# Copies of h in the last four units of a gated MLP beside attention: two parts each, at once

## The chip, the cores and the metric

The kernel runs on one core of one Trainium2 chip. The metric is the device time of that core in microseconds, here the median of three runs. Every number of the profile comes from one execution that the hardware profiler recorded.

## What is computed

An attention block and a bilinear gated MLP share one normalised input; the MLP gates the attention.

```python
xn = layernorm(x)                                  # x: 2048 x 576
q, k, v = split(xn @ wqkv)                         # 32 heads of 18
s = concat(softmax(q @ k.T * 18 ** -0.5) @ v) @ wo
h = (xn @ w_gate) * (xn @ w_up)                    # 2048 x 4608
g = silu(h @ w_down)
return x + s * g
```

All of it is in fp32. Where the kernel needs the accuracy, it splits a number into a rounded high part and a rest and adds three products (high by high, high by rest, rest by high).

## The kernel before

**Tiles and streams.** The MLP goes in 72 units: four chunks of 512 tokens by 18 blocks of 256 hidden columns (`units`). A unit has two halves, n = 2u and 2u + 1, of 128 hidden columns each. TensorE's 128 rows are used as two halves of 64 rows, each with a stream of its own: stream 0 gives the up products and stream 1 the gate products (27 matmuls a half, 512 columns, line 703), and both give down products (48 a unit, 288 columns, line 749). The order in each stream is: gate or up of unit u, then the down products of unit u − 1. Where both streams have work, their matmuls overlap.

**Where h goes.** At the end of a gate half (`gate_end`) VectorE multiplies gate and up (L715), ScalarE writes the high part of h to `hs` (L719) and GpSimd the rest (L720). The down products sum over 64 rows at a time, so each stream needs both halves of the rows: one lies in `hs`, the other in `hx`, a copy of `hs` with its upper and lower 64 partitions exchanged. SyncE issues that copy as two DMAs (`turn_round`, L739). For units 1 to 69 the copy of unit u is issued in `down_end`, behind the last down product of unit u − 1 in both streams, since there is one buffer `hx`; the load of wd for unit u (`d_get`, L240) is issued just ahead of it. For units 70 and 71 the copy goes in two parts, one at the end of each gate half, unit 70 into a buffer `hxl` in the place of the first accumulators `acc` and unit 71 into `hx`.

**The attention beside it.** 2048 score products for the maxima (a, L624, on stream 0) and 2048 for the exponentials (b, L656, on stream 1, for the last head on stream 0 as well) are set between the MLP's matmuls. ScalarE takes the exponentials (L658) into 29 buffers `pt`. When seven blocks of four stand there, both streams stop for a visit: the products with V (L667, `pv_group`), which free the buffers. The last blocks go in two visits of four. When a head is whole, VectorE divides it (L679 to L684) and its rows go to DRAM (`sot`, L687); behind the last visit they are loaded again as `o` (L843) for the final product with wo (L1295), which VectorE multiplies with the gate (L1304).

**What sets the order.** The whole order of the main part is written when the program is built, by a planner (`order`, line 1157) with clocks of its own for the two streams, the engines and SyncE's queue (`moved`: bytes at 0.24 MB/us, and 2.0 us). It gives the next instruction to the stream whose clock is behind. `can_go` (line 1118) holds a stream's first down product of unit n back until `there["h", n]` and `downed[n - 1]` are past, the planner's times at which the copy of h and the load of wd have landed. A score product b is given when its goal has passed. The goals are 0.75 us apart for the last 88 (`LAST`, line 975), and they are shifted by the lead of stream 0 in issued MLP work:

```python
lean = PULL * (gone[0] - gone[1] - SKEW) * (1 if r else -1)      # line 1185; PULL 3.0, SKEW 3.0
```

A 512-column matmul counts 0.2285 us (`LONG`), a 288-column one 0.1325. SyncE issues its DMAs in the order of the program and waits at each for what it needs.

Of the kernel before, what the change touches and what calls it, by code (L numbers as in the profile page):

```python
# [40 lines left out]
def kernel(  # L41
# [564 lines left out]
    with ExitStack() as mid:  # L606
# [103 lines left out]
        def gate_end(n, ps):  # L710
            u, j = divmod(n, 2)
            if j == 0:
                hs[u] = gp.tile([128, 2, 2, 512], FR, name="hs", bufs=2)
            h32 = us.pop(n)
            nc.vector.tensor_tensor(h32, ps, h32, op=OP.mult)  # L715
            if g_after(n):
                g_get(g_after(n))
            hj = hs[u][:, j]
            nc.scalar.activation(hj[:, 0, :], h32, AF.Copy)  # L719
            nc.gpsimd.tensor_tensor(hj[:, 1, :], h32, hj[:, 0, :].bitcast(FT), op=OP.subtract)  # L720
            if u == 0 or u >= len(units) - 2:
                turn_round(u, j)

        hx = {}

        def turn_round(u, j):

            if u >= len(units) - 2:
                if j == 0 and u == len(units) - 2:
                    hx[u] = accp.tile([128, 2, 2, 512], FR, name="hxl", tag="acc")  # L730
                elif j == 0:
                    hx[u] = gp.tile([128, 2, 2, 512], FR, name="hx", bufs=1)
                js = slice(j, j + 1)
            else:
                if u or j == 0:
                    hx[u] = gp.tile([128, 2, 2, 512], FR, name="hx", bufs=1)
                js = slice(0, 2) if u else slice(j, j + 1)
            for r in range(2):
                nc.sync.dma_start(hx[u][half[r], js].bitcast(FT), hs[u][half[1 - r], js].bitcast(FT))  # L739
# [28 lines left out]
        def down_end(r, u, s, ps):  # L768
            c, q = units[u]
            cs = slice(r * HALF, (r + 1) * HALF)  # L770
            if q == 0 and c >= 2:
                ready(sdone, 4 * c - 8 + s)
            a = sums(4 * c + s)[:, cs]
            if q == 0:
                nc.vector.tensor_copy(a, ps[:, 0:HALF])  # L775
            else:
                nc.vector.tensor_tensor(a, a, ps[:, 0:HALF], op=OP.add)  # L777
            if q == NF2 - 1 and c < NCH - 1:
                seen[c, s] = seen.get((c, s), 0) + 1
                if seen[c, s] == 2:  # L780
                    silu_store(4 * c + s)
            if s == 3:
                seen[u] = seen.get(u, 0) + 1
                if seen[u] == 2:
                    d_get(u + 1)
                    if u + 1 < len(units) - 2:
                        turn_round(u + 1, 1)

        def silu(t, new, end):
# [367 lines left out]
        def order():  # L1157
            nonlocal na, nb
            load_v(0)
            g_get(2)  # L1160
            feeds = [stream(0), stream(1)]
            heads.extend(next(f) for f in feeds)
            wait = None
            while any(heads) or na < TOTAL or nb < TOTAL or due:
                now = max(clk)
                small(now)
                if nb == TOTAL and not lo:
                    begin()
                if nb == TOTAL and len(banks["g"]) == 4:
                    banks["g"] += [max(banks["a"])] * 2  # L1170
                if loads and queue[0] <= now + 0.3:
                    f, a, size_mb = loads.pop(0)
                    f(*a)
                    moved(now, size_mb)
                need = size(due[0]) if due and (nb < TOTAL or any(heads) and not stuck[0]) else 1
                if len(due) >= need and due[need - 1][2] <= now:
                    wait = now if wait is None else wait
                    if abs(clk[0] - clk[1]) < 0.04 or now > wait + 1.0 or not all(heads):
                        visit(now if any(heads) else max([now] + [d[2] for d in due]))
                        wait = None  # L1180
                        if nb == TOTAL and not due:
                            prefetch(now)
                        continue
                r = 0 if clk[0] <= clk[1] else 1
                lean = PULL * (gone[0] - gone[1] - SKEW) * (1 if r else -1)

                if r == 0 and (na < TOTAL or nb < TOTAL - N) or r == 1 and nb == 0 and na < N:
                    at, goal, score, can = next_free("a"), a_goal(na) + lean, a_next, na < TOTAL and na < nb + N + MOST and stacked(0, na)
                    can = can and not late(goal, r)
                    at += LOAD if goal > clk[r] - BEHIND else 0.0  # L1190
                else:
                    at, goal, score, can = next_free("b"), b_goal(nb) + lean, b_next, b_ready(r)
                op = heads[r]
                held = op is not None and not can_go(r, op[1], op[4])
                stuck[0] = held and heads[1 - r] is not None and not can_go(1 - r, heads[1 - r][1], heads[1 - r][4])
                if held:
                    op = None
                blocked = op is not None and op[1] and next_free("g") > clk[r]
                if can and (at <= clk[r] + 0.01 and (goal <= clk[r] or blocked) or op is None and (at <= clk[r] or not held)):
                    clk[r] = max(clk[r], at)  # L1200
                    score(r)
                elif op is not None:
                    length, first, work, end, (kind, n, k) = op
                    if first:
                        clk[r] = max(clk[r], next_free("g"))
                        slots[r] = banks["g"].index(next_free("g"))
                        banks["g"][slots[r]] = 1e9
                    work()
                    lands = issue(r, length)
                    gone[r] += length  # L1210
                    if end:
                        done = engine(end[0], lands, end[1])
                        banks["g"][slots[r]] = done + EARLY
                        if kind == "d":
                            if k == 47:
                                parts.setdefault(n, []).append(clk[r])
                                if len(parts[n]) == 2:
                                    downed[n] = moved(max(parts[n]) + 0.3, 1.18) if (n + 1) % NF2 and n + 2 < len(units) else 0.0
                                    if n + 3 < len(units):
                                        there["h", n + 1] = moved(max(parts[n]) + 1.0, 1.05)  # L1220
                        elif r == 0:
                            upped[n] = done
                        else:
                            gated[n] = done
                            fin = engine("ACT", done + 0.05, 0.535)
                            fin = engine("POOL", fin + 0.05, 1.29)
                            if n != 2:
                                anew = 4 * NF2 - UNSAVED <= g_after(n) < 4 * NF2
                                loaded[g_after(n) - 2] = moved(done - 0.4, 1.18) if (n // 2 + 1) % NF2 and not anew else 0.0
                            if n // 2 >= len(units) - 2:  # L1230
                                there["h", n // 2] = moved(fin, 0.524) - (0.0 if n // 2 < len(units) - 1 else 1.1)
                            elif n < 2:
                                there["h", 0] = moved(fin, 0.524)
                            for _ in range(2):
                                hot = n + 2 >= 2 * NF2 and n % (2 * NF2) in (34, 35, 0) and n + 2 < 2 * len(units)
                                for want in stacks:
                                    if hot and (want[0] is load_pair or n % (2 * NF2) == 2 * NF2 - 1):
                                        continue
                                    stacks.remove(want)
                                    send(want, fin + 1.4)  # L1240
                                    break
                    heads[r] = next(feeds[r], None)
                else:
                    clk[r] = max(clk[r] + 0.05, min(clk[1 - r] + 0.01, clk[r] + 0.3))
# [120 lines left out]
```

## Time and profile before

| | |
|---|---|
| median of 3 runs | 2565.24 us |
| lowest and highest | 2562.74 and 2565.86 us |
| profiled execution | 2566.68 us |
| its span in the trace | 2564.9 us |
| matmuls busy | 2544.2 us (99%) |
| weight loads busy | 2115.4 us (82%) |
| VectorE busy | 1933.2 us (75%) |
| ScalarE busy | 1473.1 us (57%) |
| granted TensorE clock | 0.999 |

Times in the trace count from the start of the span. PE is TensorE's matmuls, PEld its weight loads, DVE VectorE, ACT ScalarE, POOL GpSimd, and SPq the queue of SyncE, which issues most DMAs. L703 is line 703 of the kernel. A name such as `hx<-hs` says what is written from what.

### The profile page before, as it was taken

How to read it: one execution, taken by the hardware profiler on the slowest of the kernel's cores; microseconds unless marked ns; L12 is line 12 of the kernel's file. 1: busy time of each engine (PE TensorE's matmuls, PEld its weight loads, DVE VectorE, ACT ScalarE, POOL GpSimd, SP SyncE). 2: the span in 40 equal slices, each digit the busy share in tenths (PEclk: the TensorE clock that was granted, in tenths of full speed). 3: DMA queues.
4: the chain of work that ended last, by engine and by line, in shares of the span. 5: the costliest groups of instructions: out<-in, count | busy, mean ns of one | idle time of the engine just before them, and what ended most of it. 6: DMA issues, size and time to landing. Idle time of an engine off the chain costs nothing.

```text
span 2564.9 us, 59227 instructions
## 1 busy us (share of the span) xinstructions
PE 2544.2 (99%) x24360; PEld 2115.4 (82%) x24360; DVE 1933.2 (75%) x3377; ACT 1473.1 (57%) x2712; POOL 618.9 (24%) x687
## 2 busy tenths in 40 slices
PE   8999999999999999999999999999999999999998
PEld 7899888787888888878888888778888888888878
DVE  6208678877778888777878888777889887778537
ACT  5222666666666655556666665555656656556651
POOL 3214334443421111112311111111111121111125
PEclk9999999999999999999999999999999999999999
DMA  7796889889775656576766566565666666664567
GB/s 246 234 293 163 222 220 244 222 217 248 199 222 173 183 174 185 173 183 186 214 201 174 172 178 184 168 178 154 180 204 164 175 190 176 178 175 142 160 194 248
DMA packets 203979, 499.87 MB, mean 195 GB/s; under 512 B 57744, under 2 KB 125200, under 8 KB 165948
## 3 DMA queue, kind: packets, MB, share of 16 engines
q1 hardware_dynamic: 193020, 482.86, 66.7%
q0 software_dynamic: 9952, 11.74, 1.7%
q8 instruction: 192, 3.15, 0.5%
q10 hardware_dynamic: 736, 1.47, 0.2%
q14 instruction: 79, 0.65, 0.1%
HBM read 307.49 MB, written 107.61 MB: 162 GB/s over the span
## 4 chain that ended last, share of the span: by engine, by line
PE 95%; DMA 2%; DVE 2%; ACT 0%; SPq 0%; POOL 0%; issue 0%; ACTq 0%; DVEq 0%
PE pg L703 35%; PE pg L667 17%; PE pg L749 15%; PE pa L624 11%; PE pb L656 9%; PE pg L423 2%; PE pa L368 2%; PE pb L368 2%; PE pg L1295 1%; DVE mx L626 0%; DMA sqk<-hl 0%; PE pa L1295 0%; PE pb L1295 0%; DMA hx<-hs 0%; DMA xi<-in_A_x_dram 0%; DMA gin<-sg 0%
## 5 line engine op out<-in xcount | busy, mean ns | idle before, releaser
L626 DVE TENSOR_REDUCE mx<-pa 128x1 f32<-128x512 f32 x2048 | 1364.7, 686 | 222.7 <-PE pa L624 114.1
L658 ACT ACTIVATE pt<-pb 128x512 f32<-128x512 f32 x2048 | 1160.8, 598 | 532.9 <-PE pb L656 477.2
L703 PE MATMUL pg<-xc,wgu 64*128 64x512 f32 x7722 | 1358.1, 388 | 0.0
L703 PEld LDWEIGHTS pg<-xc,wgu 64*128 64x128 f32 x7722 | 1048.2, 184 | 36.0 <-DVE acc L775 0.2
L656 PE MATMUL pb<-pair,ring 64*128 64x512 f32 x2016 | 784.6, 395 | 2.6 <-DMA pair<-mt 2.6
L624 PE MATMUL pa<-pair,ring 64*128 64x512 f32 x2008 | 778.2, 393 | 1.1 <-DVE mx L626 1.1
L749 PE MATMUL pg<-wd,hs 64*128 64x288 f32 x3408 | 582.2, 292 | 0.3 <-DVE acc L777 0.2
L749 PE MATMUL pg<-wd,hx 64*128 64x288 f32 x3360 | 567.7, 292 | 0.0
L749 PEld LDWEIGHTS pg<-wd,hs 64*128 64x128 f32 x3408 | 489.0, 185 | 5.5 <-issue 0.8
L720 POOL TENSOR_TENSOR hs<-us,hs 128x512 fp32r<-128x512 f32 x144 | 186.3, 1293 | 1262.6 <-ACT hs L719 1251.5
L749 PEld LDWEIGHTS pg<-wd,hx 64*128 64x128 f32 x3360 | 477.9, 185 | 3.0
L667 PE MATMUL pg<-pt,vt 128*32 128x512 f32 x4096 | 454.8, 594 | 1.0 <-DVE acc L777 0.9
L624 PEld LDWEIGHTS pa<-pair,ring 64*128 64x128 f32 x2008 | 364.9, 184 | 68.3 <-issue 51.1
L656 PEld LDWEIGHTS pb<-pair,ring 64*128 64x128 f32 x2016 | 366.0, 184 | 9.5 <-issue 2.9
L667 PEld LDWEIGHTS pg<-pt,vt 128*32 128x32 f32 x4096 | 125.5, 110 | 284.7 <-issue 278.3
L777 DVE TENSOR_TENSOR acc<-acc,pg 128x288 f32<-128x288 f32 x544 | 231.6, 443 | 26.4 <-PE pg L749 22.7
L673 DVE TENSOR_TENSOR oc<-oc,pg 128x512 f32<-128x512 f32 x69 | 47.2, 685 | 217.3 <-PE pg L667 217.2
L719 ACT ACTIVATE hs<-us 128x512 fp32r<-128x512 f32 x144 | 91.0, 632 | 140.2 <-DVE us L715 139.2
L206 POOL TENSOR_TENSOR wgu<-wraw,wgu 128x384 fp32r<-128x384 f32 x129 | 129.5, 1020 | 98.3 <-ACT wgu L205 81.5
L671 ACT ACTIVATE oc<-pg 128x512 f32<-128x512 f32 x32 | 19.1, 598 | 188.3 <-PE pg L667 181.8
L646 POOL DMA_DIRECT2D pair<-mt x128 | 77.9, 614 | 178.5 <-DVE mt L641 171.9
L715 DVE TENSOR_TENSOR us<-pg,us 128x512 f32<-128x512 f32 x144 | 98.5, 684 | 26.3 <-PE pg L703 18.0
(147 smaller groups left out, 1394.4 us busy)
## 6 DMA issues: line engine op xcount, KB each, us to landing
wgu<-swg SPq DMA_DIRECT2D x94, 1152.0 KB
hx<-hs SPq DMA_DIRECT2D x138, 512.0 KB
wd<-swd SPq DMA_DIRECT2D x50, 1152.0 KB
swg<-wgu SPq DMA_DIRECT2D x36, 1152.0 KB
pair<-sqk SPq DMA_DIRECT2D x192, 144.0 KB
ring<-sqk SPq DMA_DIRECT2D x384, 72.0 KB
swd<-wd SPq DMA_DIRECT2D x18, 1152.0 KB
sqk<-hl SPq DMA_DIRECT2D x32, 512.0 KB
```

The lines of the kernel that those rows point to most:

```text
L206: nc.gpsimd.tensor_tensor(w[:, 9 + b:12 + b, :], raw[:, b:b + 3, :], w[:, b:b + 3, :].bitcast(FT), op=OP.subtract)
L368: nc.tensor.matmul(p, wq[b, a], xcs[c][:, e, :], start=n == 0, stop=n == len(PAIRS) - 1)
L624: nc.tensor.matmul(p, q[rows, t * 128:(t + 1) * 128], k[rows, c * 512:(c + 1) * 512], start=True, stop=True)
L626: nc.vector.tensor_reduce(mx[h][:, t, c:c + 1], p, axis=AX.X, op=OP.max)
L656: nc.tensor.matmul(p, k[rows, t * 128:(t + 1) * 128], q[rows, c * 512:(c + 1) * 512], start=True, stop=True)
L658: nc.scalar.activation(pt[t, c], p, AF.Exp, scale=scale)
L667: nc.tensor.matmul(p[32 * c:32 * c + 32, :], vt[h // 2][:, t, 6 * (h % 2):6 * (h % 2) + 32], pt[t, c], start=t == ts[0], stop=t == ts[-1])
L703: nc.tensor.matmul(ps, gw[n][half[r], a, :], xg[i][half[r], e, :], start=k == 0, stop=k == len(TERMS) - 1)
L715: nc.vector.tensor_tensor(h32, ps, h32, op=OP.mult)
L720: nc.gpsimd.tensor_tensor(hj[:, 1, :], h32, hj[:, 0, :].bitcast(FT), op=OP.subtract)
L749: nc.tensor.matmul(ps[:, 0:HALF], (hx if k else hs)[u][half[r], j, a, s * 128:(s + 1) * 128], dw[u][half[r], k, j, e, :], start=n == 0, st ...
L777: nc.vector.tensor_tensor(a, a, ps[:, 0:HALF], op=OP.add)
```

## The change

The copy of h in two parts, one at the end of each gate half, now holds for the last four units (68 to 71), not the last two. The even ones of them go into the buffer of the first accumulators, the odd ones into `hx`. The planner's times for the copies follow.

```diff
-            if u == 0 or u >= len(units) - 2:
+            if u == 0 or u >= APART:
                 turn_round(u, j)
 
         hx = {}
+        APART = len(units) - 4
 
         def turn_round(u, j):
 
-            if u >= len(units) - 2:
-                if j == 0 and u == len(units) - 2:
+            if u >= APART:
+                if j == 0 and u % 2 == 0:
                     hx[u] = accp.tile([128, 2, 2, 512], FR, name="hxl", tag="acc")
                 elif j == 0:
                     hx[u] = gp.tile([128, 2, 2, 512], FR, name="hx", bufs=1)
...
                 if seen[u] == 2:
                     d_get(u + 1)
-                    if u + 1 < len(units) - 2:
+                    if u + 1 < APART:
                         turn_round(u + 1, 1)
...
                                     downed[n] = moved(max(parts[n]) + 0.3, 1.18) if (n + 1) % NF2 and n + 2 < len(units) else 0.0
-                                    if n + 3 < len(units):
+                                    if n + 1 < APART:
                                         there["h", n + 1] = moved(max(parts[n]) + 1.0, 1.05)
...
-                            if n // 2 >= len(units) - 2:
+                            if n // 2 >= APART:
                                 there["h", n // 2] = moved(fin, 0.524) - (0.0 if n // 2 < len(units) - 1 else 1.1)
```

## Rows read from the trace of the kernel before

**Rows 1.** The page, section 1: busy us (share of the span) xinstructions.
```profile
PE 2544.2 (99%) x24360; PEld 2115.4 (82%) x24360; DVE 1933.2 (75%) x3377; ACT 1473.1 (57%) x2712; POOL 618.9 (24%) x687
```
**Rows 2.** Windows: busy us (xinstructions) of PE, PEld, DVE, ACT, POOL, clock, DMA share, GB/s.
```profile
2430.20:2440.70 10.50, 10.50 (x101) 10.46 (x98) 0.85 (x2) 8.88 (x18) 0.00 (x0) 1.00 0.69 184
2440.80:2443.70 2.90, 2.90 (x16) 2.35 (x13) 0.69 (x1) 2.52 (x5) 1.29 (x1) 1.00 0.94 243
```
**Rows 3.** TensorE in order of time from 2440.8: start us, us, instructions merged.
```profile
2440.83 0.84 PE L703 MATMUL pg<-xc,wgu 64*128 64x512 f32 x3
...
2443.75 0.40 PE L749 MATMUL pg<-wd,hs 64*128 64x288 f32 x1
```
**Rows 4.** TensorE in order of time from 2412.1.
```profile
2412.13 0.39 PE L656 MATMUL pb<-pair,ring 64*128 64x512 f32 x1
...
2413.05 0.39 PE L749 MATMUL pg<-wd,hs 64*128 64x288 f32 x1
```
**Rows 5.** SyncE's queue in order of time, units 68 and 69 and the tail.
```profile
2386.73 1.06 SPq L265 DMA_DIRECT2D ring<-sqk  x3
2402.32 0.34 SPq L240 DMA_DIRECT2D wd<-swd  x1
2402.77 1.40 SPq L739 DMA_DIRECT2D hx<-hs  x2
...
2418.61 1.05 SPq L265 DMA_DIRECT2D ring<-sqk  x3
2432.63 0.34 SPq L240 DMA_DIRECT2D wd<-swd  x1
2433.09 1.11 SPq L739 DMA_DIRECT2D hx<-hs  x2
...
2487.81 2.94 SPq L687 DMA_DIRECT2D sot<-oc  x4
```
**Rows 6.** Windows behind three issues of copies; the last number is GB/s.
```profile
2403.20:2412.90 9.70, 9.70 (x86) 9.53 (x83) 1.92 (x6) 6.44 (x12) 5.88 (x9) 1.00 1.14 247
2433.50:2443.10 9.60, 9.60 (x77) 9.13 (x74) 0.69 (x1) 8.03 (x16) 0.80 (x1) 1.00 1.00 259
2477.70:2480.20 2.50, 2.50 (x33) 2.42 (x31) 0.44 (x1) 1.89 (x4) 0.00 (x0) 1.00 0.98 247
```
**Rows 7.** Waits of SyncE's queue, 2380 to 2520: us in total, times, longest.
```profile
SPq L739 <- POOL hs L720: 11.6, 4, 4.3
SPq L687 <- DVE oc L684: 3.9, 1, 3.9
```
**Rows 8.** TensorE in order of time: the first product of the last head's exponentials.
```profile
2416.90 0.47 PE L656 MATMUL pb<-ring,pair 64*128 64x512 f32 x1
```
**Rows 9.** GpSimd in order of time: the last silu that reads the first accumulators.
```profile
2094.14 1.42 POOL L805 TENSOR_TENSOR sil<-sil,acc 128x576 f32<-128x576 f32 x1 [8.05 <-DVE sil L802]
```
**Rows 10.** Windows of pt alone: PE, PEld and ACT busy (x); ACT is the exponentials.
```profile
2405.50:2412.00 6.50, 0.00 (x0) 0.00 (x0) 2.78 (x5) 1.00 1.08 256
2412.00:2416.90 4.90, 0.00 (x0) 0.00 (x0) 3.46 (x7) 1.00 0.92 208
2428.10:2448.80 20.70, 0.02 (x3) 0.02 (x4) 15.49 (x28) 1.00 0.69 191
```
**Rows 11.** The chain that ended last, in order of time: start us, us, what.
```profile
2483.01 8.33 DMA hx<-hs
...
2491.41 0.34 SPq L843
...
2513.25 0.47 DVE ys L1304
```
**Rows 12.** TensorE in order of time, the final products; in brackets the idle time.
```profile
2513.86 1.03 PE L1295 MATMUL pa<-wos,hi 128*128 128x288 f32 x6 [1.22 <-DVE ys L1304]
```
**Rows 13.** ScalarE in order of time, the last exponentials.
```profile
2474.85 3.85 ACT L658 ACTIVATE pt<-pb 128x512 f32<-128x512 f32 x6
2479.07 0.60 ACT L658 ACTIVATE pt<-pb 128x512 f32<-128x512 f32 x1
```

## The prediction

> **What bounds the kernel now.** The page's busy times come first: the matmul row is full nearly from end to end, and everything else is below it [rows 1]. That says only that TensorE never stands empty, not that it works at its full rate, since two matmuls on the two halves of its rows overlap. So the second view is the busy times by windows round the units that the diff touches, cut so that no visit of the P·V products lies in them. The reader is to look at the weight loads (PEld) in it. With both streams at work 98 of them take 10.5 us, 107 ns each; from 2440.8 on 13 take 2.9 us, 223 ns each, though the matmul row is full in both [rows 2]. Here one stream runs alone. The third view, TensorE's instructions in order of time, shows which: from 2440.83 only products of gate and of scores come, until the first down product (L749) at 2443.75 [rows 3]. The same is seen in small from 2412.13 to 2413.05 [rows 4]. The fourth view, SyncE's queue, says why. The copy of h of units 68 and 69 is issued only when the down products of the unit before are all through, behind the load of wd: wd at 2402.32 and the copy at 2402.77, wd at 2432.63 and the copy at 2433.09 [rows 5]. Both together are 1.18 + 1.05 = 2.23 MB, and at the 247 and 259 GB/s of the windows that follow they take 9.0 and 8.6 us [rows 6]. From the start of those windows that is 2412.2 and 2442.1, close ahead of the two first down products. The planner has counted the same (`there["h", ...]`), and holds the down products of stream 0 back until then. So the profile has two holds that this change can remove, 0.92 and 2.92 us of one stream.
>
> A rule bears on how such a hold is priced. In the longer one the matmul row is busy 2.90 us of 2.90, the weight loads 2.35 [rows 2]. The Trainium skill (Perfetto Trace Analysis, section Identifying the Most-Contended Engine) calls the first no good measure of the distance to the roofline and the second a good one. By the first the hold would be worth 0, by the second 2.90 − 2.35 = 0.55 us; the count of loads, 223 ns apart against 107, gives half of the hold, 1.5 us, and the trace decides for the count.
>
> **What the change does, part by part.** Ahead of unit 68 no line of the program differs, so nothing moves before its gate halves, the second of which stands ahead of the load of ring at 2386.73 [rows 5]. Only the last 190 us are in play.
>
> (a) *Copies of units 68 and 69 go early.* They leave at the ends of the gate products as those of unit 70 do today, and no longer after the down products of the unit before. They are there more than 15 us ahead of their use. Both holds go: half of 0.92 and half of 2.92 us, −0.5 and −1.5, together **−1.9 us of TensorE** (rounded from 1.92).
>
> What is late next at those places is wd. Alone its 1.18 MB need 1.18/0.247 = 4.8 us from 2403.2, so 2408.0, and 1.18/0.259 = 4.6 us from 2433.5, so 2438.1 [rows 6]. Stream 0 arrives at 2412.1 and 2440.8; the slack is 4 and 2.7 us. By the planner's own sum (0.3 + 1.18/0.24 + 2.0 = 7.2 us after the down products) the second is 2439.8, 1.0 us ahead. I cost that at nothing, at most 1 us of one stream, 0.5 us, if stream 0 leads by more.
>
> (b) *Four issues of 256 KB in place of two of 512 KB a unit.* SyncE needs 1.11 us for two, so 2.2 us more in all. SyncE also now waits there for GpSimd's subtraction, as in the four waits of units 70 and 71 (11.6 us in all, the longest 4.3) [rows 7]. Queued behind are the loads of ring for head 31, today at 2386.73 and 2418.61 [rows 5]; they go at most 4.3 + 1.1 = 5.4 us later. The first product of head 31 with those rows comes at 2416.90 [rows 8], and the second half of ring is wanted 32 products later, beyond 2440 by 0.74 us each. The cover is 24 and 16 us; without it each microsecond would go to the score products. Cost 0. The halves are no slower for their bytes: 247 GB/s for a pair of halves, 259 GB/s for the two whole ones with wd [rows 6].
>
> (c) *The other buffer.* hx of unit 68 takes the place of the first accumulators, last read by the last silu of the third chunk, which GpSimd ends at 2095.56 [rows 9], 280 us before. hx of 69 takes that of 67, whose down products are through at 2402.3. Neither is a wait. Cost 0.
>
> (d) *The planner's pace of score products.* No wait and no instruction is added here, but it is the term that I think decides. Stream 1 gives a score product whenever its goal is due, and the goal is put off by 3 us for each microsecond by which stream 0 has issued more than stream 1 (line 1185). While stream 0 runs freely, each product on stream 1 costs it 0.2285 us, so the pace is 0.75 + 3 × 0.2285 = 1.44 us a product. The trace shows five exponentials in 6.5 us ahead of the hold, 1.30 each, and seven in 4.9 us once stream 0 is held [rows 10]. The hold itself buys them: 3 × 0.92 = 2.8 us of goal. Without it, 4.9/1.30 = 3.8 products fit into those 4.9 us, so **3 products are put off**. From 2416.9 on both streams may give products of head 31, and the pace is that of ScalarE and two score banks: 28 in 20.7 us, 0.74 each [rows 10]. Nothing there is idle enough to catch up, so the last exponential comes 3 × 0.74 = **2.2 us later**. The bounds: nothing, if they are caught up; 7 × 1.30 − 4.9 = 4.2 us, if all seven go at the old pace.
>
> (e) *What ends the tail.* Behind the last product the last P·V visit, its division, the stores of head 31's rows (2487.81, where the queue waited 3.9 us for VectorE) and the loads of o (2491.41) follow one after the other, and the chain runs on through gin, xi and o to 2513.25 [rows 5, 7, 11]. TensorE already waits 1.22 us there [rows 12]. So the 1.9 us of (a) do not reach the end: earlier down products only make that wait longer. What they bring is that the copy of unit 71, which lands at 2491.34 [rows 11] and holds the first load of o, is out of the way by the stores' end, today 2487.81 + 2.94 = 2490.75: −0.6 us. Bounds of that: 0 and −1.9.
>
> **The sum.** −1.9 us on TensorE, absorbed by the wait of (e); +2.2 by (d); −0.6 by (e): +1.6 us. The profiled execution took 2566.68 us (span 2564.9 and 1.8 around it), 1.4 above the median of 2565.24; it would come to 2568.3, and the median to **2566.8 us**. That is 0.06%, and 0.2% (5.1 us, about what a measurement of this kernel can tell from no change) is beyond all the terms but one bound.
>
> **The rivals.**
> *The gain arrives.* If the score products are caught up, or stream 0 takes more of them, the last exponential comes 1.9 us earlier with everything else: 2565.2 − 1.9 = 2563.3. For it: the planner balances the streams, and the last products stand on both. Against: ahead of the last exponential, which ends at 2479.67, ScalarE gives six of them end to end in 3.85 us, so it has no room there to be sooner [rows 13]. The Trainium skill (Perfetto Trace Analysis, section DMA Optimizations) says that DMAs split into smaller chunks may start sooner and let the whole task end sooner; it would give this rival; the rows bear it out for the two holds, and none does for the end.
> *Slower.* All seven products go at 1.30 us, head 31 begins 4.2 us late, and at the end gate and up are done while products remain: they run alone at half rate, half of 4.2 − 1.9, so 1.1 us more. 4.2 + 1.1 = +5.3: 2570.5. It decides from four put-off products on. For it: stream 0's lead feeds on itself through line 1185. Against: from 2416.9 on stream 0 takes products too, which ends it.
> *It does not do what it says.* With more lead, stream 0 meets the load of wd (slack 1.0 us by the planner) or of the next gate weights, and is held there instead: 0, so 2565.2.
>
> **How the numbers follow.** Forecast 0.45, gain 0.27, slower 0.18, held elsewhere 0.10. The forecast and the last one are within 0.2%; of the gain, 0.05 is for a last stretch that also closes its 1.22 us wait and more; of the slower case two thirds, 0.12, lie beyond 0.2%, since its 5.3 us leave out what is lost when visits move too. So faster 0.05, same 0.83, slower 0.12. The range reaches from the gain, less half the distance of the shown runs' lowest from their median (2565.24 − 2562.74 = 2.50), so 2562.0, to the slower case, 2570.5.
>
> **What would show it.** In the trace after: no stretch of L703 and L656 alone ahead of the first down products of units 68 and 69 (a); four copies at gate ends, ring issued behind them (b); exponentials still about 1.3 us apart between 2412 and 2417, and a next P·V visit that begins later than before (d); the first load of o behind head 31's stores (e). If that visit begins earlier or the last exponential ends before 2479.67, (d) is wrong and the gain arrives. If the loads of o move and the end does not, (e) is wrong.

## The result, and the profile after

The changed kernel takes 2572.82 us (median of 8 runs, 2567.73 to 2574.42), the kernel before 2564.62 (8 runs): a ratio of 1.003, 95% interval 1.0022 to 1.0039. It is slower by 8.2 us, and above the range of the prediction. The profiled execution of the changed kernel took 2570.59 us, with a span of 2568.8. That is 2.2 us below its median, and the profiled execution of the kernel before (2566.68 us) lies 2.1 above its own. So the two traces are 3.9 us apart, and they show the cause at work but only about half of the 8.2 us.

The two holds are gone. Windows of the changed kernel at the places of [rows 2] (columns as there): the weight loads now fill the stretch round unit 69's first down products (the first begins at 2439.93), 28 in 2.9 us against 13.

```profile
2430.70:2437.30 6.60, 6.60 (x61) 6.24 (x61) 0.45 (x1) 6.11 (x12) 0.00 (x0) 1.00 0.60 212
2437.40:2440.30 2.90, 2.90 (x30) 2.90 (x28) 0.69 (x1) 2.10 (x5) 1.10 (x1) 1.00 0.49 153
```

TensorE in order of time, to be held against [rows 4]: the first down products of unit 68 now follow the dense gate and up products at once.

```profile
2410.46 1.52 PE L703 MATMUL pg<-xc,wgu 64*128 64x512 f32 x11
2411.73 0.39 PE L656 MATMUL pb<-pair,ring 64*128 64x512 f32 x1
2411.82 0.42 PE L750 MATMUL pg<-wd,hs 64*128 64x288 f32 x2
```

SyncE's queue, to be held against [rows 5]: the copies go in parts behind the loads of gate weights, and a load of ring waits behind one of them (2390.04, before 2386.73). Head 31's stores come at 2494.38, before 2487.81, and the loads of o behind them.

```profile
2380.60 1.10 SPq L740 DMA_DIRECT2D hxl<-hs  x2
2385.97 0.33 SPq L197 DMA_DIRECT2D wgu<-swg  x1
2388.89 1.10 SPq L740 DMA_DIRECT2D hxl<-hs  x2
2390.04 2.02 SPq L265 DMA_DIRECT2D ring<-sqk  x3
...
2494.38 1.37 SPq L687 DMA_DIRECT2D sot<-oc  x4
2495.99 2.28 SPq L844 DMA_DIRECT2D o<-sot  x5
```

The exponentials alone by windows, as in [rows 10] (the last bracket before the clock is their count): 5 in 4.9 us in the place of the seven, then 9 (one of them begun before) in 7.7 us until the next P·V visit, which begins at 2424.3. Behind that visit 28 take 22.1 us, before 20.7.

```profile
2405.10:2411.60 6.50, 0.00 (x0) 0.00 (x0) 2.77 (x5) 1.00 0.43 114
2411.60:2416.50 4.90, 0.00 (x0) 0.00 (x0) 2.48 (x5) 1.00 0.91 318
2416.50:2424.20 7.70, 0.00 (x0) 0.00 (x0) 4.49 (x9) 1.00 0.74 224
2430.60:2452.70 22.10, 0.00 (x0) 0.00 (x0) 15.76 (x28) 1.00 0.66 219
```

And here is what the prediction did not see. ScalarE in order of time, to be held against [rows 13]: the last gate half is over at 2476, ScalarE then issues the six loads of wo, and 13 exponentials (4 + 2 + 4 + 3) stand behind them in its queue. The first waits 3.56 us. Before, those issues came at 2480.55, behind the last exponential.

```profile
2475.11 1.08 ACT L658 ACTIVATE pt<-pb 128x512 f32<-128x512 f32 x2 [3.34 <-PE pb L656]
2476.14 0.63 ACT L719 ACTIVATE hs<-us 128x512 fp32r<-128x512 f32 x1
2476.15 1.84 ACTq L826 DMA_DIRECT2D wor<-in_A_wo_dram  x4
2478.03 2.26 ACTq L828 DMA_DIRECT2D wor<-in_A_wo_dram  x2
2480.34 2.27 ACT L658 ACTIVATE pt<-pb 128x512 f32<-128x512 f32 x4 [3.56 <-DMA wor<-in_A_wo_dram]
2482.78 1.09 ACT L658 ACTIVATE pt<-pb 128x512 f32<-128x512 f32 x2 [0.17 <-PE pb L656]
2484.03 2.32 ACT L658 ACTIVATE pt<-pb 128x512 f32<-128x512 f32 x4 [0.15 <-PE pb L656]
2486.52 1.78 ACT L658 ACTIVATE pt<-pb 128x512 f32<-128x512 f32 x3 [0.17 <-PE pb L656]
```

TensorE stands as well, for 3.31 us until the first of these exponentials is through; down products go on at that moment too, which fits a queue in order whose head waits for a score bank. In the windows it has 0.01 us of work between 2478 and 2481. After the last down product it waits for o, and from 2500 to 2506.8 the granted clock is 0.50, the lower of its two levels, 1.2 GHz.

```profile
2480.99 0.49 PE L656 MATMUL pb<-ring,pair 64*128 64x512 f32 x1 [3.31 <-ACT pt L658]
2480.99 0.40 PE L750 MATMUL pg<-wd,hs 64*128 64x288 f32 x1
...
2478.00:2481.00 3.00, 0.01 (x2) 0.01 (x2) 0.00 (x0) 0.66 (x2) 0.13 (x1) 1.00 0.98 302
2497.60:2500.00 2.40, 0.79 (x6) 0.37 (x2) 1.63 (x4) 0.88 (x2) 0.00 (x0) 0.99 0.92 278
2500.00:2506.80 6.80, 6.21 (x24) 5.67 (x24) 1.96 (x2) 2.00 (x4) 4.59 (x3) 0.50 0.98 281
```

The chain of waits, to be held against [rows 11] and [rows 12]: it goes through the issues of wo and the exponential behind them, which the chain before does not, and then through the load of o, the rounding of o on ScalarE and the final products at half clock.

```profile
2476.58 0.44 ACTq L826
2477.07 3.27 DMA wor<-in_A_wo_dram
2480.34 0.61 ACT pt L658
...
2495.99 3.12 DMA o<-sot
2499.12 0.63 ACT hi L852
...
2500.90 3.01 PE pa L1296 x10
```

Three places measure the tail. The early parts of the executions differ by up to 4 us, so I count each from the start of the P·V visit near 2391 us, which stands ahead of every matmul and exponential that the change moves (the times are read from the order of time):

| from that visit, us | last exponential ends | product of the last gate half begins (L715) | last final product begins |
|---|---|---|---|
| before | 88.0 | 88.1 | 166.7 |
| changed | 97.0 | 84.1 | 171.5 |

Before, the first two lie within 0.1 us of each other. The change moves the MLP 4.0 us forward and the exponentials 9.0 us back.

### The profile page after: what moved, and what is told of

Same layout as the page of the kernel before. It is cut to its first block, busy times and chain, and to the rows that moved or that the text cites. A ratio compares the mean times of both kernels' runs of the same rounds, so it can differ in the third digit from the quotient of the medians.

```text
span 2568.8 us, 59234 instructions
## 1 busy us (share of the span) xinstructions
PE 2545.2 (99%) x24360; PEld 2114.8 (82%) x24360; DVE 1931.2 (75%) x3377; ACT 1472.0 (57%) x2712; POOL 617.3 (24%) x687
## 4 chain that ended last, share of the span: by engine, by line
PE 96%; DVE 2%; DMA 1%; ACT 0%; POOL 0%; issue 0%; ACTq 0%; DVEq 0%; SPq 0%
PE pg L703 35%; PE pg L667 18%; PE pg L750 16%; PE pa L624 11%; PE pb L656 9%; PE pg L423 2%; PE pa L368 2%; PE pb L368 2%; PE pg L1296 1%; PE pa L1296 1%; PE pb L1296 1%; DVE mx L626 0%; DMA sqk<-hl 0%; DMA pair<-mt 0%; DVE st L298 0%; DVE us L715 0%
## 5 line engine op out<-in xcount | busy, mean ns | idle before, releaser
L750 PE MATMUL pg<-wd,hx 64*128 64x288 f32 x3312 | 558.3, 292 | 0.0
L750 PEld LDWEIGHTS pg<-wd,hx 64*128 64x128 f32 x3312 | 470.1, 185 | 2.9
L715 DVE TENSOR_TENSOR us<-pg,us 128x512 f32<-128x512 f32 x144 | 98.5, 684 | 20.8 <-PE pg L703 18.9
```

The lines of the kernel that those rows point to most:

```text
L750: nc.tensor.matmul(ps[:, 0:HALF], (hx if k else hs)[u][half[r], j, a, s * 128:(s + 1) * 128], dw[u][half[r], k, j, e, :], start=n == 0, st ...
```

## The experiments

Each run is compared with the kernel before on the same chip; intervals are 95%.

**Copies or order.** Two halves of the change. First the copies alone:

```diff
-                                    if n + 1 < APART:
+                                    if n + 3 < len(units):
...
-                            if n // 2 >= APART:
+                            if n // 2 >= len(units) - 2:
```

> The changed kernel with the planner's two lines as before: the copies of units 68 and 69 go early and in parts, but every matmul and every exponential stands in the order of the kernel before, the down products held back included. Theory 'order': the loss of 8.2 us lies in the new order alone, so this is the time of the kernel before, 2564.6 us, within 2 us. Rival 'copies': the extra issues, SyncE's waits for GpSimd or the shared buffer cost, so this stands near the changed kernel's 2572.8 us.

Measured: 2564.97 us, ratio 1.000 (0.9991 to 1.0009). Then the kernel before with the changed planner's times alone:

> The kernel before with the planner's two lines of the change: the matmuls and exponentials stand in the order of the changed kernel, but the copies of units 68 and 69 still go whole and behind the down products of the unit before. Theory 'order': 2572.8 us and up to 4 us more, since the first down products of units 68 and 69 now wait on the chip for a copy that lands late (0.9 and 2.9 us in the trace of before). Rival 'copies': near 2564.6 us.

Measured: 2573.30 us, ratio 1.0038 (1.0025 to 1.0051). So the loss is in the order. The four copies, SyncE's waits for GpSimd, the late load of ring and the shared buffer cost nothing beyond the interval of 0.1% either way, as the prediction's (b) and (c) had it.

**The six issues on ScalarE.** The changed kernel with one word altered in each of the two lines that load wo (the first is shown):

```diff
-                nc.scalar.dma_start(wov["raw"][:, k, :], wo[128 * k:128 * k + 128, :])
+                nc.sync.dma_start(wov["raw"][:, k, :], wo[128 * k:128 * k + 128, :])
```

> The changed kernel with the six loads of wo issued by SyncE in place of ScalarE, at the same place of the program. In the trace of the changed kernel ScalarE issues them from 2476.15 to 2480.29 while 13 exponentials are still to come, and stands still for 3.56 us. Theory 'exponentials behind the issues': the last exponential comes some 4 us sooner and the low clock of 6.8 us goes in part, so 2566 to 2569 us. Rival 'pace of products alone': the issues stand beside other waits, and the time stays within 1.5 us of 2572.8.

Measured: 2565.00 us, ratio 1.0006 (0.9997 to 1.0015): 7.8 us less than the changed kernel, 0.8 more than the kernel before beside it, and a little below the range that I gave. ScalarE in order of time shows the exponentials without the wait. The issues themselves take SyncE about as long, 3.7 us, but nothing is computed there:

```profile
2473.69 0.63 ACT L719 ACTIVATE hs<-us 128x512 fp32r<-128x512 f32 x1
2474.23 1.07 ACT L658 ACTIVATE pt<-pb 128x512 f32<-128x512 f32 x2
2475.46 1.10 ACT L658 ACTIVATE pt<-pb 128x512 f32<-128x512 f32 x2 [0.17 <-PE pb L656]
...
2476.92 2.60 SPq L826 DMA_DIRECT2D wor<-in_A_wo_dram  x4
2479.56 1.14 SPq L828 DMA_DIRECT2D wor<-in_A_wo_dram  x2
```

That SyncE is a better place for any order would explain it as well, so the same step on the kernel before:

> The kernel before with the six loads of wo issued by SyncE. In its order no exponential stands behind them. If the gain of 7.8 us that the changed kernel has from this step lies in the exponentials behind the issues, it brings nothing here: within 1.5 us of 2564.5. Rival: SyncE is the better place for any order, and this is 3 us or more faster.

Measured: 2564.39 us, ratio 0.9999 (0.9990 to 1.0008). It brings nothing that can be seen where no exponential stands behind.

The issues left on ScalarE, but behind the exponentials (`wo_load`, with the planner's entry for its bytes, is called when the last score product has been given):

> The changed kernel with the six loads of wo still issued by ScalarE, but behind the last 13 exponentials, not ahead of them; no other instruction moves on ScalarE. Theory 'exponentials behind the issues': the 3.6 us go as in the run with the issues on SyncE, less what the later loads of wo cost at the final product (they are issued near 2482, as in the kernel before at 2480.5): 2565 to 2568 us. Rival 'a queue's load': if the run with SyncE gained by where the bytes come from or when they move, this stays at 2571 to 2574 us.

Measured: 2569.08 us, ratio 1.0021 (1.0012 to 1.0029). Near half comes back, less than I expected. The wait is gone, and the last exponential ends 93.5 us from the visit, as with SyncE (93.4). But the last P·V visit begins 94.7 us from it, against 92.7 with SyncE, since the planner now sets down products of unit 71 ahead of it, and the clock is low for 10.2 us behind. The load of o that the chain of waits goes through is longer too, 5.09 us against 3.17. What each of these costs was not separated. So taking the wait away in this manner brings 3.7 us, and the rest of what SyncE brings is not traced to one cause.

The disputed cost by itself, in the kernel before, and its counterpart with SyncE as the issuer (`spare` is a new DRAM tensor of six rows):

```diff
+                                if r and n == 2 * len(units) - 2:
+                                    for i in range(6):
+                                        nc.scalar.dma_start(spare[i:i + 1, :], wo[i:i + 1, :])
```

> The kernel before with six small DMAs more (a row of wo each, to DRAM that nothing reads) issued by ScalarE at the end of unit 71's first gate half, with seven exponentials behind them in its queue. This is the disputed cost by itself, without the copies and without the new order. Theory 'exponentials behind the issues': six issues of 0.45 us take 2.7 us, the last exponential comes 2 to 3.5 us later, and the time is 2566.5 to 2569, with the low clock up to 3 us more. Rival: the issues hide beside other work, within 1.5 us of 2564.2.

> The kernel before with the same six small DMAs at the same place, issued by SyncE and not by ScalarE. Six of them on ScalarE cost 8.6 us. Theory 'exponentials behind the issues': the DMAs themselves are nothing, so this is within 2 us of the kernel before, 2563 to 2566.5. Rival 'the DMAs disturb the queue's loads': they still delay the copy of unit 71 and the loads behind them, 2569 to 2574.

Measured: on ScalarE 2573.18 us, ratio 1.0033 (1.0021 to 1.0046), which is 8.6 us for six DMAs of 2.3 KB; on SyncE 2566.72 us, ratio 1.0010 (1.0001 to 1.0020). Some six microseconds are thus ScalarE's queue, and 2.7 us, a little more than I allowed, are left for the DMAs themselves and SyncE's queue. I had put the issues at 0.45 us each. They took 1.0, and everything on ScalarE stood behind them. Here the last gate half comes as late as the last exponential, 95.0 and 94.9 us from the visit, 7 us behind the kernel before:

```profile
2473.64 6.00 ACTq L910 DMA_DIRECT2D spare<-in_A_wo_dram  x6
2479.68 1.09 ACT L659 ACTIVATE pt<-pb 128x512 f32<-128x512 f32 x2 [5.42 <-DMA spare<-in_A_wo_dram]
```

**The pace of the products.** If late products are the cause, earlier goals must cure it. Three ways: without the lead of stream 0, with goals 4.8 us earlier, and with the first hold put back in the order alone:

```diff
-                lean = PULL * (gone[0] - gone[1] - SKEW) * (1 if r else -1)
+                lean = PULL * (gone[0] - gone[1] - SKEW) * (1 if r else -1) if na < TOTAL else 0.0
```

> The changed kernel, in which the planner leaves the lead of stream 0 out of the goals of score products once the maxima are all through (from about 2403 us). Products then come 0.75 us apart from there on, not 1.3 to 1.6. Theory 'pace': the last exponential is ahead of the last gate product again, nothing stands behind the loads of wo, and the 1.9 us of the two holds may arrive: 2562 to 2565 us. Rival 'copies': 2572.8 us. Rival 'loads of wo alone': if the exponentials still end behind them, 2569 to 2572 us.

```diff
                     at, goal, score, can = next_free("b"), b_goal(nb) + lean, b_next, b_ready(r)
+                    goal -= 4.8 if na == TOTAL else 0.0
```

> The changed kernel with the goals of score products 4.8 us earlier once the maxima are through, in place of the goal that the hold used to give. By that no exponential stands behind the loads of wo on ScalarE, while stream 0's lead still counts. Theory 'late products in front of a fixed place': the time of the kernel before or up to 2 us less, 2562 to 2565.5. Rival: the run that left the lead out (2572.8) shows that any hastening of the products costs the MLP as much at the end; then 2569 to 2573.

```diff
-                                    if n + 1 < APART:
+                                    if n + 1 < APART + 1:
...
-                            if n // 2 >= APART:
+                            if n // 2 >= APART + 1:
```

> The changed kernel with the planner's time for unit 68's copy as before and that for unit 69's as changed; both copies go early. So the first hold (0.92 us of stream 0) stays in the order and the second (2.92 us) goes. In this order no exponential stands behind ScalarE's issues of the loads of wo. Theory 'the first hold bought the early products': the time of the kernel before or up to 2 us less, 2562.5 to 2565. Rival 'any removed hold unbalances the end': 2567 to 2572.

Measured: 2572.78 (1.0038, 1.0025 to 1.0050), 2573.89 (1.0038, 1.0026 to 1.0051) and 2573.34 us (1.0035, 1.0021 to 1.0048). My theory of the early products fell in all three. The first run lands on the number of the rival 'copies', which the copies alone had already ruled out. In the other two the rival that hastened products cost the MLP as much at the end has the right side, and both lie above the range that I gave it. The exponentials do end early enough (82.5, 86.3 and 87.6 us from the visit), but products that come sooner take the gate's place on stream 1: the product of its last half begins at 94.3, 94.1 and 95.0, six to seven us late. Then the copy of unit 71 and the loads of wo are late, and TensorE waits for the copy. No exponential stands behind the issues of wo here, so these losses have another cause than that of the changed kernel. In the run with the first hold kept:

```profile
2498.93 1.09 PE L750 MATMUL pg<-wdl,hx 64*128 64x288 f32 x6 [9.04 <-DMA hx<-hs]
```

The other half, the first hold removed and the second kept in the order:

> The other half: unit 68's copy with its changed time, unit 69's with the time of before. The first hold goes, the second stays. Five exponentials stand behind ScalarE's issues. Theory 'the first hold bought the early products': slower, 2567 to 2572, between the changed kernel and the one before. Rival 'the second, longer hold matters more': 2564 to 2566.

Measured: 2573.98 us, ratio 1.0035 (1.0022 to 1.0047), 2 us above what I gave: the last exponential at 96.5, five of them behind the issues. With the issues on ScalarE neither hold could be taken out by itself.

Both cures together, goals 2.8 us earlier and wo on SyncE:

> The changed kernel with goals 2.8 us earlier (what the first hold gave, 3 x 0.92) and the loads of wo on SyncE. Theory: the products are as early as in the kernel before and nothing stands behind ScalarE's issues, so the two holds' 1.9 us can show: 2561.5 to 2564. Rival 'the tail waits for DMA anyway': 2564.5 to 2566, no better than with SyncE alone.

Measured: 2565.02 us, ratio 1.0005 (0.9996 to 1.0014). The ends lie at 89.5 and 86.0, nearly together again, and the two holds' 1.9 us do not show: the second expectation held in its number.

**The low clock.** Twenty matmuls that nothing reads, ahead of the first final product:

```diff
+    last = dw[len(units) - 1]
+    for i in range(20):
+        nc.tensor.matmul(ps[1][1][:, 0:HALF], last[:, 0, 0, 0, 0:128], last[:, 0, 0, 1, :], start=True, stop=True)
```

> The changed kernel with the loads of wo on SyncE and 20 matmuls more that nothing reads, between the last down product and the first final product, where TensorE stands idle for about 2.5 us before its clock falls to 0.5 for 6.8 us. Theory 'the gap brings the low clock': the low clock goes and with it half of 6.8 us, less at most 0.5 us for the matmuls: 2561.5 to 2563.5. Rival 'the clock falls for what lies earlier (the narrow P.V loads, the idle time near 2478)': the low clock stays and the time is 2565 to 2567.5.

> The changed kernel with 20 matmuls more that nothing reads ahead of the first final product, where TensorE waits and its clock falls to 0.5 for 6.8 us. Theory 'the low clock is a part of the loss': it falls later or not at all, and 2 to 3.4 us come back: 2569 to 2571. Rival 'the stretch waits for loads of o anyway' (as where it brought nothing with the loads of wo on SyncE): 2572 to 2574.5.

Measured with wo on SyncE: 2566.01 us, ratio 1.0005 (0.9997 to 1.0014). The clock stays at 1.00 there, where without the twenty it was 0.51 from 2494 to 2501. So the gap did bring the low clock, against the second expectation, but the number is the second's: no gain is seen. In the trace ScalarE's roundings of o wait for loads of o round that stretch, 5.68 and 6.02 us. And the run without the twenty, low clock included, is only 0.8 us from the kernel before.

On the changed kernel itself: 2572.53 us, ratio 1.0031 (1.0019 to 1.0042). There the low clock only moved, to 2480 to 2486.8, behind TensorE's wait for the exponentials. The second expectation held there. How much of the 8.2 us the low clock is stays open. The most that 6.8 us at half clock can be is 3.4 us, but that is the profiled execution. Over the eight runs of the changed kernel the time goes with the clock: 2567.73 us at a mean clock of 0.999, 2570.59 and 2570.67 at 0.998, 2572.51 to 2574.42 at 0.996 and 0.997. A clock lower by 0.001 over the whole span is 2.6 us of TensorE (an estimate from 2568.8 us), so the slower executions have more of the low clock than the trace shows. Whether it makes them slow or comes with longer waits, no run separates.

## Why the prediction was wrong

**The holds (a): right.** Both are gone from the places where they were read. Their price, 1.9 us, is seen at the end of no run.

**Queue, copies, buffer (b, c): right.** The copies alone measured 2564.97, 0.75 us from the kernel before beside them.

**The pace (d): right in kind, and the step that failed in size.** "3 products are put off": 5 exponentials in 4.9 us where 7 were, so two, and the next visit begins 2.9 us later, counted from the visit before (2424.3 − 2391.3 = 33.0 us, before 2421.8 − 2391.7 = 30.1). Up to there the 2.2 us stand nearly. But "the last exponential comes 2.2 us later" was 9.0. Some 2.5 us more were lost by the later blocks (9.0 − 2.9 − 3.56), and 3.56 us by something that the step did not list at all: I asked what the put-off products wait for, not what they would fall behind. ScalarE's issues of the loads of wo are tied to the last gate half. As that moved forward by 4.0 us and the exponentials back, they changed places. The prediction has no row for those issues, though they stood in the trace before, 0.88 us behind the last exponential's end.

**The tail (e): right in kind.** The loads of o stand behind head 31's stores, 4.6 us later (2495.99 against 2491.41, or 5.0 counted from the visit), and the last final product is 4.8 us later from the visit. Its −0.6 us for the copy of unit 71 no run shows. But it was not tied to the exponentials alone, as (e) has it. With wo on SyncE the exponentials end 5.4 us late (93.4 from the visit) and the median is 0.8 us from the kernel before; with the exponentials on time and the gate six to seven us late (the first hold kept) it is 8.4 us slower. Before, the chain that ended last ran through the copy of unit 71 [rows 11], which fits that the exponentials had room. So the failed step is (d)'s last exponential, 2.2 us forecast and 9.0 measured, of which 3.56 are the wait behind the six issues. For the mechanism that the forecast did price, the run with wo on SyncE is the nearest: +0.8 us, with an interval from −0.8 to +3.8, in which the +1.6 lies.

**The rivals.** *Slower* had the right sign, and products did remain when gate and up were done, as it said: 13 exponentials. But the put-off was two products and not seven, the products ran beside down products and not alone, and without the issues on ScalarE 7.8 us of the loss are gone. *The gain arrives* fell: even with the issues out of the way the 1.9 us are not seen, in 2565.00 and 2565.02 us. The rule of the Trainium skill named there (Perfetto Trace Analysis, section DMA Optimizations) says that smaller chunks may let the whole task end sooner if the DMA engines are generally idle. The prediction left that condition out, and here the DMA engines are not idle: their share round the holds was 0.69 to 1.14 [rows 2, 6]. The split copies alone left the time where it was.

**What stays open.** The low clock's share, and why the medians of changed kernel and wo on SyncE lie 7.8 us apart when the wait on ScalarE is 3.56. In the two traces 3.6 us are the exponentials (97.0 against 93.4), and as much is seen at the last final product (171.5 against 168.0). Another 2.4 us lie ahead of the visit near 2391 (2391.30 against 2388.85), where the two programs do not differ, so they come from the execution and not from the edit. The last 2.0 us lie between the profiled executions and their medians (2.2 for the changed kernel, 0.2 for the other), where the changed kernel's clock is lower in most runs than in its trace. That the wait on ScalarE costs is thus shown, but its price in the traces is about half of the difference between the medians.

## What to carry to other kernels

Where a change lets one chain run ahead of another, list everything that each engine's queue holds at the place of the meeting, DMA issues included: here ScalarE began no activation until its six issues were through, and their place is fixed by the program, not by need. The holds of 0.92 and 2.92 us stood in a tail whose two ends met within 0.1 us. That such a stall may hold two chains in step, and that removing it pays only if what stands at the joint can move, is a reading that these runs suggest and do not prove. When goals or holds are altered in a planned order, measure the order without the data movement and the data movement without the order.

## What the runs showed of the hardware

Six DMA issues on ScalarE took 4.1 us for the loads of wo and 6.0 us for six of 2.3 KB each. An activation that began with the first of them ran its 0.63 us; no other ran until the last was issued. On SyncE the same loads of wo took 3.7 us and the six small ones 4.8 us, while an issue of its copies took 0.55 us. In the changed kernel TensorE's granted clock fell to 0.50 for 6.8 us after TensorE had stood idle for 3.3 us near 2478 and for 1.6 us between 2497.6 and 2500; with the later gap filled it fell at the earlier one. With wo on SyncE, where no idle time near 2478 stands, it fell as well, to 0.51 from 2494 to 2501, after 1.7 us of idle time in two pieces. And TensorE's busy row was full, 2.90 of 2.90 us, in a hold in which weight loads came at half their rate, 223 ns apart against 107.
